# Softmax weights of the first three token groups on VectorE, and the values' low part ahead of the minima

## The chip, the cores and the metric

The kernel runs on one core of a Trainium2 chip. The metric is the time of one execution on the device, in microseconds (us); before the change it is 902.17 us, the median of three runs (901.9, 902.17 and 903.5). Nothing else runs on the core, and all inputs and outputs lie in HBM.

## The reference

Attention with a sliding window and a linear position bias, then two feed-forward layers over all tokens:

```python
scores = (q @ k^T) / sqrt(64)                # 4 batches, 8 heads, 576 positions, head size 64
scores = where(0 <= i - j < 128, scores - slope[h] * |i - j|, -1e9)
attn = exp(scores - max(scores)); attn /= sum(attn) + 1e-9
x = (attn @ v) as 2304 tokens x 512
h = x @ w_in;  x = (h * clip(h + 3, 0, 6) / 6) @ w_out        # 512 -> 2048 -> 512
h = x @ w_in2; out = (s * max(h, 0)**2 + b) @ w_out2           # 512 -> 2048 -> 512
```

All of it is float32, and the feed-forward products are made from two parts of each number: a high part rounded to the matmul's own type (fp32r) and the low part that is left.

## The kernel before

**Groups, units and steps.** The tokens are cut into eight groups of 256 or 320: groups 0 to 3 hold the first two blocks of 128 rows of each batch, groups 4 to 7 the rest. `NATIVE` is 2: groups 0 and 1 are computed by `StartUnit`, the others by `Unit`. A unit is one head of one group; two heads (an even and an odd one) form a pair and share the loads, and each of the two classes has the same stages: scale the queries, scores (TensorE), minima (VectorE, which also adds the bias and masks), exponentials (ScalarE, with the row sums as a second output), `sums` (VectorE: 1e-9 is added and the reciprocal taken), `weights` (the exponentials are multiplied with the reciprocals, on GpSimd), transposes (TensorE), copies into SBUF, values (TensorE), `to_hi` (ScalarE) and `to_lo` (VectorE), which leave the high and low part of the attention's result in the group's `x` tile. Beside the units run the steps of the first feed-forward layer: `Step(t, f)` computes for group `t` and block `f` of 128 hidden columns the product `h`, then ScalarE and VectorE form `g` and split it, then the product `o`. The matmuls of `h` need VectorE's `product` of the step before, since `h` has one PSUM bank.

**The weights.** The first layer's weights come in as raw numbers and are unpacked and split on the chip: `Half` does this in the first 130 us on ScalarE (`high`, L229 and L230; `hi`, L249), VectorE (`sign`, a shift at L234 and a bit operation at L237; `lo`, L253) and GpSimd (`add`, L243). The second layer's weights follow later in `Pair`.

**The order.** It is written out by hand: `at(slot, rank, fn)` puts a function into a slot at a rank, and slots and ranks are gone through in order; each engine gets its instructions in that order and works through them in order. Units of groups 0 and 1 take one slot each (unit `i` has its minima in slot `i`, its sums and weights in slot `i + 1`, its transposes in slot `i + 4`). From slot 13 on the steps take the even or odd slots, and the pairs of the later groups are eight slots apart, so that a group's units run beside the steps of the groups before. Within a slot the ranks that matter here are: 30.1 `high`, 30.4 `to_hi`, 31 `add` and `lo`, 31.5 `product`, 32 minima, 32.1 `lower`, 32.2 and 33 sums, exponentials and weights, 38 `sign`, 39 `to_lo`.

**Buffers.** The scores, transposes and values of `Unit` share three PSUM banks (tag `a`); a bank is free again when its last reader is done: the minima for the scores, `to_hi` and `to_lo` for the values. A unit's statistics (minimum, sum, reciprocal; up to five columns each) lie in a small tile `st` with four buffers. During the first slots TensorE also runs warm-up matmuls whose result nobody reads.

Of the kernel before, what the change touches and what calls it, by code (L numbers as in the profile page):

```python
# [8 lines left out]
F32 = mybir.dt.float32  # L9
# [5 lines left out]
ALU = mybir.AluOpType  # L15
# [8 lines left out]
def tile_alibi_window_attention_moe_moe2(  # L24
# [52 lines left out]
    def at(slot, rank, fn):  # L77
        plan.setdefault(slot, []).append((rank, len(plan[slot]), fn))
# [193 lines left out]
    attn_ctx = ExitStack()  # L272
    ap = attn_ctx.enter_context(tc.tile_pool(name="ap", bufs=2))

    def rows(i):
        return min(P, S - i * P)


    class Unit:
# [11 lines left out]
        def plan(self, s):  # L291
# [22 lines left out]
            if odd:  # L314
                at(s + 17, 20, self.values)
                at(s + 18, 30.4, self.to_hi)
                at(s + 18, 39, self.to_lo)

        def pair(self):
            return units[self.g * H + self.h // 2 * 2 :][:2]  # L320
# [62 lines left out]
        def minima(self):  # L383
            even = self.pair()[0]
            if even is self:
                self.st = ap.tile([P, 3, 5], F32, tag="st", bufs=4, name=f"st{self.id}")
            self.st = even.st
            self.Pt = ap.tile([P, 3, P], F32, tag="P", bufs=5, name=f"P{self.id}")
            for i in range(self.qa, self.two):
# [31 lines left out]
            self.exp(2, 4)  # L421

        def sums(self):
            n, st = 4 + (self.two < self.qb), self.st
            nc.vector.tensor_scalar(
                out=st[:, 2, :n], in0=st[:, 1, :n], scalar1=1e-9, scalar2=None, op0=ALU.add
            )
            nc.vector.reciprocal(st[:, 2, :n], st[:, 2, :n])  # L428

        def weight(self, i, c):  # L430
            pt = self.Pt[:, i]
            nc.gpsimd.tensor_scalar(  # L432
                out=pt, in0=pt, scalar1=self.st[:, 2, c : c + 1], scalar2=1.0,
                op0=ALU.mult, op1=ALU.mult,
            )

        def weights(self):
            for i in range(self.qa, self.two):
# [77 lines left out]
    class StartUnit(Unit):  # L516
# [36 lines left out]

        def scale(self):

            for u in self.pair():
                c = -(D ** -0.5) / slopes[u.h]
                if self.g + u.h == 0:
                    nc.vector.tensor_scalar(
                        out=u.X, in0=u.raw[u.p, :256], scalar1=c, scalar2=None, op0=ALU.mult  # L560
                    )
                elif self.g + self.h == 0:
                    nc.scalar.activation(u.X, u.raw[u.p, :256], AF.Copy, scale=c)
                else:
                    nc.gpsimd.tensor_scalar(
                        out=u.X, in0=u.raw[u.p, :256], scalar1=c, scalar2=1.0,
                        op0=ALU.mult, op1=ALU.mult,
                    )

        blocks = ((0, 0, P), (1, P, 3 * P))  # L570

# [10 lines left out]

        def minima(self):
            self.Pt = ap.tile([P, 3 * P], F32, tag="P", bufs=5, name=f"P{self.id}")
            self.st = ap.tile([P, 3, 5], F32, tag="st", bufs=4, name=f"st{self.id}")
            for i, a, b in self.blocks:
                nc.vector.tensor_tensor_reduce(  # L587
                    out=self.Pt[:, a:b], in0=self.ps[:, a:b], in1=rel2[:, 2 * P - (b - a) :],
                    scale=slopes[self.h], scalar=3.0e38, op0=ALU.add, op1=ALU.min,
                    accum_out=self.st[:, 0, i : i + 1],  # L590
                )
# [6 lines left out]
                )  # L598

        def sums(self):  # L600
            nc.vector.tensor_scalar(
                out=self.st[:, 2, :2], in0=self.st[:, 1, :2], scalar1=1e-9, scalar2=None, op0=ALU.add
            )
            nc.vector.reciprocal(self.st[:, 2, :2], self.st[:, 2, :2])

        def weights(self):
            for i, a, b in self.blocks:
                nc.gpsimd.tensor_scalar(
                    out=self.Pt[:, a:b], in0=self.Pt[:, a:b], scalar1=self.st[:, 2, i : i + 1],
                    scalar2=1.0, op0=ALU.mult, op1=ALU.mult,  # L610
                )

        def transposes(self):
# [719 lines left out]
```

## Time and profile before

| | before |
|---|---|
| median of three runs | 902.17 us |
| the profiled execution | 902.07 us, of which the span from first to last instruction is 900.4 |
| TensorE busy (matmuls) | 877.4 us, 97% |
| VectorE | 624.7 us, 69% |
| ScalarE | 521.6 us, 58% |
| GpSimd | 341.7 us, 38% |

The names in the profile are PE for TensorE's matmuls and PEld for its weight loads, DVE for VectorE, ACT for ScalarE, POOL for GpSimd and SP for the engine that issues the DMAs. A row of a timeline has the start, the duration, the engine, the line of the kernel, the operation, what it writes and reads, and in brackets how long the engine sat idle before it and what ended that. Busy shares are means over stages that have different limits.

### The profile page before, as it was taken

The numbers are of one execution on the slowest core, as the hardware profiler recorded it, in microseconds if no ns is written. First come the engines' busy times: TensorE is split into PE (matmuls) and PEld (weight loads), VectorE is DVE, ScalarE is ACT, GpSimd is POOL, SyncE is SP. The second block draws the span as 40 slices with busy tenths as digits, with TensorE's granted clock in tenths as the row PEclk, the third lists the DMA queues.
The fourth block names the chain that finished last, engine by engine and source line by source line (L and its number), as shares of the span: only waits on it lengthen the run. The fifth ranks groups of instructions, "written<-read, shape, count | busy, mean of one in ns | idle before, by whom it ended". The sixth has DMA issues, their size and how long they took to land.

```text
span 900.4 us, 17714 instructions
## 1 busy us (share of the span) xinstructions
PE 877.4 (97%) x6469; PEld 836.4 (93%) x6469; DVE 624.7 (69%) x1376; ACT 521.6 (58%) x1227; POOL 341.7 (38%) x526
## 2 busy tenths in 40 slices
PE   9799899999999999999999999999999999999998
PEld 4589889899999999999999999999999999999998
DVE  7899885665787667776765745778747787476672
ACT  7888775555665556556555435665446656266551
POOL 7834541323554544454442311444104440144300
PEclk9999999999999999999999999999999999999999
DMA  9454332427466546454447335887779777777772
GB/s 336 134 174 136 112 106 89 160 65 231 139 210 205 170 148 216 161 180 165 170 170 257 141 165 183 297 299 263 274 237 327 274 270 268 256 259 261 281 258 94
DMA packets 66823, 183.19 MB, mean 203 GB/s; under 512 B 9904, under 2 KB 29616, under 8 KB 58288
## 3 DMA queue, kind: packets, MB, share of 16 engines
q1 hardware_dynamic: 66736, 182.06, 59.1%
q8 instruction: 51, 0.84, 0.4%
q14 instruction: 36, 0.29, 0.1%
HBM read 143.13 MB, written 38.80 MB: 202 GB/s over the span
## 4 chain that ended last, share of the span: by engine, by line
PE 84%; DVE 7%; ACT 4%; DMA 2%; issue 2%; SPq 0%; POOL 0%; ACTq 0%; POOLq 0%
PE o L1062 20%; PE h L1122 19%; PE h L672 19%; PE o L710 18%; PE v L497 3%; PE s L368 2%; DMA raw<-w 2%; PE t L453 1%; DVE staging_early L234 1%; DVE g L697 1%; ACT staging_early L229 1%; DVE raw L237 1%; PE s L376 1%; DVE P L587 1%; DVE t L686 1%
## 5 line engine op out<-in xcount | busy, mean ns | idle before, releaser
L710 PE MATMUL o<-g,w 128*128 128x256 f32 (+1 forms) x1536 | 234.2, 301 | 1.1 <-DVE g L697 0.9
L672 PE MATMUL h<-x,w 128*128 128x256 f32 (+1 forms) x1536 | 226.8, 296 | 7.9 <-DVE t L686 7.6
L710 PEld LDWEIGHTS o<-g,w 128*128 128x128 f32 x1536 | 210.8, 189 | 10.8 <-issue 4.2
L672 PEld LDWEIGHTS h<-x,w 128*128 128x128 f32 x1536 | 211.3, 189 | 10.2 <-DVE t L686 9.5
L1062 PE MATMUL o<-wstream,i 128*128 128x256 f32 x1512 | 180.4, 281 | 0.0
L1062 PEld LDWEIGHTS o<-wstream,i 128*128 128x128 f32 x1512 | 180.0, 188 | 0.0
L1122 PE MATMUL h<-x,wstream 128*128 128x384 f32 x1008 | 176.7, 334 | 0.0
L1122 PEld LDWEIGHTS h<-x,wstream 128*128 128x128 f32 x1008 | 174.4, 188 | 0.2
L683 ACT ACTIVATE t<-h 128x256 f32<-128x256 f32 (+1 forms) x128 | 52.4, 409 | 141.5 <-PE h L672 141.1
L686 DVE SCALAR_TENSOR_TENSOR t<-t,h 128x256 f32<-128x256 f32 (+1 forms) x128 | 57.7, 451 | 80.2 <-ACT t L683 79.7
L697 DVE TENSOR_TENSOR g<-t,g 128x256 fp32r<-128x256 f32 (+1 forms) x128 | 67.2, 525 | 34.6 <-ACT g L693 32.6
L482 POOL TENSOR_SCALAR_AFFINE_SELECT W<-F 128x128 f32<-128x128 f32 (+1 forms) x144 | 46.8, 359 | 108.6 <-ACT F L457 104.5
L1156 ACT ACTIVATE g<-g,scalar 128x384 f32<-128x384 f32 x96 | 58.6, 610 | 39.4 <-DVE g L1141 37.0
L432 POOL TENSOR_SCALAR P<-P,st 128x128 f32<-128x128 f32 x112 | 57.1, 524 | 41.6 <-DVE st L428 40.5
L693 ACT ACTIVATE g<-t 128x256 fp32r<-128x256 f32 (+1 forms) x128 | 56.3, 440 | 28.5 <-DVE t L686 28.2
L1179 POOL TENSOR_TENSOR g<-g 128x384 f32<-128x384 f32 x24 | 24.3, 1015 | 117.7 <-PE h L1122 98.8
L1140 DVE TENSOR_TENSOR g<-h,s 128x384 f32<-128x384 f32 x72 | 39.8, 553 | 31.3 <-PE h L1122 22.5
L919 DVE SCALAR_TENSOR_TENSOR i<-g,scalar,i 128x768 fp32r<-128x768 f32 x48 | 49.3, 1077 | 11.7 <-ACT i L918 11.7
L1091 ACT ACTIVATE u<-o 128x256 f32<-128x256 f32 x36 | 13.2, 385 | 73.1 <-PE o L1062 73.1
L1141 DVE SCALAR_TENSOR_TENSOR g<-g 128x384 f32<-128x384 f32 x72 | 47.3, 658 | 2.5
L918 ACT ACTIVATE i<-g,scalar 128x768 fp32r<-128x768 f32 x48 | 41.5, 926 | 6.4 <-PE o L1062 6.4
L1132 ACT ACTIVATE s<-h 128x384 f32<-128x384 f32 x72 | 34.7, 482 | 17.8 <-PE h L1122 17.4
(122 smaller groups left out, 1176.6 us busy)
## 6 DMA issues: line engine op xcount, KB each, us to landing
wstream<-wo SPq DMA_DIRECT2D x42, 1024.0 KB, 5.0
raw<-w SPq DMA_DIRECT2D x53, 512.0 KB, 4.9
wstream<-wh SPq DMA_DIRECT2D x24, 1024.0 KB, 5.6
wstream<-wh SPq DMA_DIRECT2D x24, 768.0 KB, 5.8
wh<-staging_early SPq DMA_DIRECT2D x16, 512.0 KB, 3.0
wo<-staging_early SPq DMA_DIRECT2D x12, 512.0 KB, 3.3
stage<-w SPq DMA_DIRECT2D x11, 512.0 KB, 4.4
out<-u SPq DMA_DIRECT2D x11, 384.0 KB, 3.0
```

What stands on the lines that cost most here:

```text
L432: nc.gpsimd.tensor_scalar(out=pt, in0=pt, scalar1=self.st[:, 2, c : c + 1], scalar2=1.0, op0=ALU.mult, op1=ALU.mult,)
L672: nc.tensor.matmul(self.ps, lhsT=w[:, wp, cc * P : (cc + 1) * P], rhs=x[:, cc, xp], start=m == 0, stop=m == 3 * CC - 1,)
L683: nc.scalar.activation(self.a, self.ps, AF.Relu, bias=3.0)
L686: nc.vector.scalar_tensor_tensor(out=self.a, in0=self.a, scalar=6.0, in1=self.ps, op0=ALU.min, op1=ALU.mult)
L693: nc.scalar.activation(self.g[:, 0], self.a, AF.Copy)
L697: nc.vector.tensor_tensor(out=self.g[:, 1], in0=self.a, in1=hi, op=ALU.subtract)
L710: nc.tensor.matmul(acc[t][d], lhsT=w[:, wp, DM + d * P : DM + (d + 1) * P], rhs=self.g[:, gp], start=f == 0 and i == 0 and (t > 1 or d % 2 ...
L919: nc.vector.scalar_tensor_tensor(out=out[:, :, 1], in0=src, scalar=b, in1=hi.bitcast(F32), op0=ALU.add, op1=ALU.subtract,)
L1062: nc.tensor.matmul(self.acc[k][c], lhsT=g[:, gp, c * P : (c + 1) * P], rhs=w[:, wp * HB : (wp + 1) * HB], start=k in (0, 1, 5) and p == 0 ...
L1122: nc.tensor.matmul(self.ps[first], lhsT=w[:, wp, cc], rhs=x[:, cc, xp], start=n == first and m == 0, stop=m == 5, skip_group_check=True,)
L1141: nc.vector.scalar_tensor_tensor(out=g, in0=g, scalar=0.0, in1=g, op0=ALU.max, op1=ALU.mult)
L1156: nc.scalar.activation(g, g, AF.Copy, scale=s_sb)
```

## The change

Four things change, and one goes with them.

- In `to_lo` of `Unit` only the place changes: rank 31.9 instead of 39 in its slot, so that VectorE has it ahead of the minima.
- `weights` of `StartUnit` (groups 0 and 1) and of group 2 (`self.g == NATIVE`) multiply on VectorE instead of GpSimd, with the same operands.
- `sums` becomes `inverse`: instead of adding 1e-9 with an immediate, a reduction over two rows of the statistics adds the sum and a row that holds 1e-9, and writes over the minimum, which the exponentials no longer need; the reciprocal follows in place. All units use it.
- In `scale` of `StartUnit` the two scalings of a pair on GpSimd, 64 partitions each with a constant, become one over 128 partitions with a column of constants; the first pair's stay on VectorE and ScalarE.
- The statistics lie in one tile with four slots, used in turn, whose row of 1e-9 GpSimd fills once.

```diff
@@ -272,6 +272,26 @@
     attn_ctx = ExitStack()
     ap = attn_ctx.enter_context(tc.tile_pool(name="ap", bufs=2))
 
+
+    NST = 4
+    sts = []
+
+    def next_st():
+        if not sts:
+            whole = ap.tile([P, NST, 3, 5], F32, bufs=1, name="st")
+            nc.gpsimd.memset(whole[:, :, 2], 1e-9)
+            sts.extend(whole[:, i] for i in range(NST))
+        sts.append(sts.pop(0))
+        return sts[-1]
+
+    def inverse(st, n):
+        total = st[:, 0, :n]
+        nc.vector.tensor_reduce(
+            out=total, in_=st[:, 1:3, :n].rearrange("p r n -> p n r"),
+            axis=mybir.AxisListType.X, op=ALU.add,
+        )
+        nc.vector.reciprocal(total, total)
+
     def rows(i):
         return min(P, S - i * P)
 
@@ -314,7 +334,7 @@
             if odd:
                 at(s + 17, 20, self.values)
                 at(s + 18, 30.4, self.to_hi)
-                at(s + 18, 39, self.to_lo)
+                at(s + 18, 31.9, self.to_lo)
 
         def pair(self):
             return units[self.g * H + self.h // 2 * 2 :][:2]
@@ -383,7 +403,7 @@
         def minima(self):
             even = self.pair()[0]
             if even is self:
-                self.st = ap.tile([P, 3, 5], F32, tag="st", bufs=4, name=f"st{self.id}")
+                self.st = next_st()
             self.st = even.st
             self.Pt = ap.tile([P, 3, P], F32, tag="P", bufs=5, name=f"P{self.id}")
             for i in range(self.qa, self.two):
@@ -421,18 +441,16 @@
             self.exp(2, 4)
 
         def sums(self):
-            n, st = 4 + (self.two < self.qb), self.st
-            nc.vector.tensor_scalar(
-                out=st[:, 2, :n], in0=st[:, 1, :n], scalar1=1e-9, scalar2=None, op0=ALU.add
-            )
-            nc.vector.reciprocal(st[:, 2, :n], st[:, 2, :n])
+            inverse(self.st, 4 + (self.two < self.qb))
 
         def weight(self, i, c):
-            pt = self.Pt[:, i]
-            nc.gpsimd.tensor_scalar(
-                out=pt, in0=pt, scalar1=self.st[:, 2, c : c + 1], scalar2=1.0,
-                op0=ALU.mult, op1=ALU.mult,
-            )
+            pt, r = self.Pt[:, i], self.st[:, 0, c : c + 1]
+            if self.g == NATIVE:
+                nc.vector.tensor_scalar(out=pt, in0=pt, scalar1=r, scalar2=None, op0=ALU.mult)
+            else:
+                nc.gpsimd.tensor_scalar(
+                    out=pt, in0=pt, scalar1=r, scalar2=1.0, op0=ALU.mult, op1=ALU.mult
+                )
 
         def weights(self):
             for i in range(self.qa, self.two):
@@ -553,19 +571,21 @@
 
         def scale(self):
 
-            for u in self.pair():
-                c = -(D ** -0.5) / slopes[u.h]
-                if self.g + u.h == 0:
-                    nc.vector.tensor_scalar(
-                        out=u.X, in0=u.raw[u.p, :256], scalar1=c, scalar2=None, op0=ALU.mult
-                    )
-                elif self.g + self.h == 0:
-                    nc.scalar.activation(u.X, u.raw[u.p, :256], AF.Copy, scale=c)
-                else:
-                    nc.gpsimd.tensor_scalar(
-                        out=u.X, in0=u.raw[u.p, :256], scalar1=c, scalar2=1.0,
-                        op0=ALU.mult, op1=ALU.mult,
-                    )
+            if self.g + self.h == 0:
+                for u in self.pair():
+                    c = -(D ** -0.5) / slopes[u.h]
+                    if u.h == 0:
+                        nc.vector.tensor_scalar(
+                            out=u.X, in0=u.raw[u.p, :256], scalar1=c, scalar2=None, op0=ALU.mult
+                        )
+                    else:
+                        nc.scalar.activation(u.X, u.raw[u.p, :256], AF.Copy, scale=c)
+            else:
+                j = self.h // 2
+                nc.gpsimd.tensor_scalar(
+                    out=self.raw[:, 768:], in0=self.raw[:, :256], scalar1=qscale[:, j : j + 1],
+                    scalar2=1.0, op0=ALU.mult, op1=ALU.mult,
+                )
 
         blocks = ((0, 0, P), (1, P, 3 * P))
 
@@ -582,7 +602,7 @@
 
         def minima(self):
             self.Pt = ap.tile([P, 3 * P], F32, tag="P", bufs=5, name=f"P{self.id}")
-            self.st = ap.tile([P, 3, 5], F32, tag="st", bufs=4, name=f"st{self.id}")
+            self.st = next_st()
             for i, a, b in self.blocks:
                 nc.vector.tensor_tensor_reduce(
                     out=self.Pt[:, a:b], in0=self.ps[:, a:b], in1=rel2[:, 2 * P - (b - a) :],
@@ -598,16 +618,13 @@
                 )
 
         def sums(self):
-            nc.vector.tensor_scalar(
-                out=self.st[:, 2, :2], in0=self.st[:, 1, :2], scalar1=1e-9, scalar2=None, op0=ALU.add
-            )
-            nc.vector.reciprocal(self.st[:, 2, :2], self.st[:, 2, :2])
+            inverse(self.st, 2)
 
         def weights(self):
             for i, a, b in self.blocks:
-                nc.gpsimd.tensor_scalar(
-                    out=self.Pt[:, a:b], in0=self.Pt[:, a:b], scalar1=self.st[:, 2, i : i + 1],
-                    scalar2=1.0, op0=ALU.mult, op1=ALU.mult,
+                nc.vector.tensor_scalar(
+                    out=self.Pt[:, a:b], in0=self.Pt[:, a:b], scalar1=self.st[:, 0, i : i + 1],
+                    scalar2=None, op0=ALU.mult,
                 )
 
         def transposes(self):
```

## Rows read from the trace of the kernel before

**Rows 1.** The page's busy time, share of the span and instructions of each engine.
```profile
PE 877.4 (97%) x6469; PEld 836.4 (93%) x6469; DVE 624.7 (69%) x1376; ACT 521.6 (58%) x1227; POOL 341.7 (38%) x526
```
**Rows 2.** Busy time by stage: stage, length, busy (instructions) by engine, clock, DMA, GB/s.
```profile
12.05:29.87 17.82, 16.53 (x113) 9.37 (x112) 17.41 (x69) 17.27 (x55) 16.92 (x29) 1.00 0.82 319
29.87:45.00 15.13, 11.16 (x72) 8.30 (x71) 12.18 (x42) 12.63 (x37) 11.47 (x15) 0.89 0.35 106
60.00:130.00 70.00, 63.80 (x522) 59.40 (x523) 62.94 (x153) 56.67 (x142) 34.24 (x41) 1.00 0.37 118
130.00:480.00 350.00, 344.23 (x2659) 326.08 (x2659) 236.71 (x685) 198.25 (x547) 149.43 (x309) 1.00 0.51 167
```
**Rows 3.** The timeline of VectorE between 8 and 40 us.
```profile
8.62 0.29 DVE L587 CUSTOM_DVE_ANT_0 P<-s,rel 128x128 f32<-128x128 f32 x1 [0.61 <-PE s L578]
...
10.90 0.43 DVE L234 TENSOR_SCALAR staging_early<-staging_early 128x512 int32<-128x512 int32 x1 [0.53 <-ACT staging_early L229]
...
12.05 0.28 DVE L587 CUSTOM_DVE_ANT_0 P<-s,rel 128x128 f32<-128x128 f32 x1
...
21.75 0.17 DVE L604 RECIPROCAL st<-st 128x2 f32<-128x2 f32 x1
21.84 0.40 DVE L512 TENSOR_TENSOR x<-v,x 128x256 fp32r<-128x256 f32 x1
...
29.87 0.28 DVE L587 CUSTOM_DVE_ANT_0 P<-s,rel 128x128 f32<-128x128 f32 x1
...
34.21 0.68 DVE L253 TENSOR_TENSOR w<-stage,w 128x512 fp32r<-128x512 f32 x1
...
36.48 0.70 DVE L601 TENSOR_SCALAR st<-st 128x2 f32<-128x2 f32 x1
...
39.78 0.42 DVE L697 TENSOR_TENSOR g<-t,g 128x256 fp32r<-128x256 f32 x1 [1.13 <-ACT g L693]
```
**Rows 4.** The timeline of ScalarE and TensorE between 30 and 35 us.
```profile
30.25 0.41 ACT L595 ACTIVATE P<-P,st 128x128 f32<-128x128 f32 x1 [0.25 <-DVE st L587]
...
34.56 0.89 PE L578 MATMUL s<-raw 64*128 64x128 f32 x6 [2.40 <-ACT W L625]
```
**Rows 5.** The timeline of GpSimd and VectorE at 31 and at 58 us.
```profile
31.63 3.53 POOL L608 TENSOR_SCALAR P<-P,st 128x128 f32<-128x128 f32 x4
...
57.81 1.04 POOL L243 TENSOR_TENSOR raw<-raw 128x512 int32<-128x512 int32 x1 [3.86 <-DVE raw L237]
...
57.86 1.27 DVE L234 TENSOR_SCALAR staging_early<-staging_early 128x512 int32<-128x512 int32 x1
```
**Rows 6.** VectorE's groups by line and shape, 10.85 to 29.9 us: busy us, mean ns.
```profile
L253 DVE TENSOR_TENSOR w<-raw,w 128x512 fp32r<-128x512 f32 x4 | 3.5, 882 | 0.0
...
L601 DVE TENSOR_SCALAR st<-st 128x2 f32<-128x2 f32 x8 | 1.8, 224 | 0.0
```
**Rows 7.** VectorE's groups by line and shape over the whole span.
```profile
L425 DVE TENSOR_SCALAR st<-st 128x5 f32<-128x5 f32 x16 | 2.6, 161 | 0.0
...
L122 DVE TENSOR_SCALAR rel<-rel 128x128 f32<-128x128 f32 x1 | 0.2, 227 | 0.0
```
**Rows 8.** The timeline of TensorE and VectorE at 220 and at 355 us.
```profile
220.62 0.41 PE L453 MATMUL t<-ident,P 128*128 128x128 f32 x2 [1.01 <-DVE st L394]
...
354.82 0.48 DVE L686 SCALAR_TENSOR_TENSOR t<-t,h 128x320 f32<-128x320 f32 x1
...
355.52 1.92 PE L672 MATMUL h<-x,w 128*128 128x320 f32 x12
```
**Rows 9.** What TensorE waited for, 60 to 130 us: us in all, times, longest.
```profile
PE h L672 <- DVE t L686: 6.6, 6, 1.7
```
**Rows 10.** The timeline of VectorE and TensorE from 78 to 81 us.
```profile
78.15 1.26 DVE L234 TENSOR_SCALAR staging_early<-staging_early 128x512 int32<-128x512 int32 x1
...
80.58 1.70 PE L672 MATMUL h<-x,w 128*128 128x256 f32 x12 [0.84 <-DVE t L686]
```
**Rows 11.** What TensorE waited for, over the whole span.
```profile
PE t L453 <- DVE st L394: 4.4, 5, 1.0
```

## The prediction

> **What bounds the kernel now.** I read the page's engine shares first, then the busy time by stage, then VectorE's instructions in the stages where it is full, and last what TensorE waited for. Over the span TensorE is busy 97% and VectorE 69% [rows 1], but that average hides two regimes [rows 2]. From 130 us on, TensorE is busy 344.23 of 350 us and VectorE 236.71: work added to VectorE there is beside TensorE's. Before that it is the other way round. From 12.05 to 29.87 us VectorE is busy 17.41 of 17.82 us, ScalarE 17.27 and GpSimd 16.92; TensorE's 16.53 is padded with warm-up matmuls. From 60 to 130 VectorE has 62.94 of 70 us, TensorE 63.80. The change puts work on VectorE exactly in these two stages, and takes it from GpSimd.
>
> The start can be read as one chain. The minima of unit 4 begin at 12.05, those of unit 12 at 29.87 [rows 3]: four pairs of units in 17.82 us, 4.46 us a pair. VectorE's rows of that stretch follow each other without a gap. ScalarE's exponentials of unit 12 start at 30.25, after 0.25 us of waiting for exactly those minima, and TensorE's scores at 34.56 wait 2.40 us for a copy that stands behind them in ScalarE's queue [rows 4]. So a microsecond more on VectorE between 12 and 30 us comes out later at TensorE, and nothing after 45 us has the room to give it back.
>
> VectorE's durations there hold waits for GpSimd. At 57.81 GpSimd's add starts and takes 1.04 us; VectorE's shift, 0.43 us when alone at 10.90 [rows 3], starts at 57.86 and takes 1.27: it ended only after the add [rows 5]. The opposite order exists too: from 31.63 four of GpSimd's multiplies took 3.53 us while VectorE ran without a gap. In the start the difference of two weights took 0.88 us in the mean against 0.68 at 34.21, and the sum's first instruction 0.224 against 0.161 [rows 3, 6, 7].
>
> **The change, part by part.** The sum is made against the profiled execution: 902.07 us, a span of 900.4 and 1.7 around it; the median of the runs is 902.17, so the two are one number here.
>
> *Weights of groups 0 and 1 (16 units).* Per unit VectorE gains one 128x128 and one 128x256 multiply, SBUF to SBUF. The trace has no such multiply on VectorE. Nearest is the 128x128 add of a constant, 0.227 us [rows 7]; for 256 columns I go a third of the way to the 0.43 of 128x512: 0.30. The other bound is one element per cycle: 0.28 for the minima's 128x128 [rows 3], and between that and 0.48 for 320 columns [rows 8] about 0.41. I take the first, as its operands lie in the same memory. VectorE's next instruction starts some 0.08 before the recorded end of the one in front (the reciprocal at 21.75 lasts 0.17, its successor starts at 21.84), so the two take 0.20 + 0.22; but the first of them needs the reciprocal's result and waits for its end, 0.11 more. That is 0.53 a unit, 1.06 a pair; by the other bound 1.4.
> What may come back: the difference of weights 0.88 to 0.68 once a pair, and the sum's 0.224 to 0.161 twice (its new form is a reduction of ten numbers at most, which I price like the old one): 0.33 a pair. GpSimd keeps one add of 1.04 and one scaling a pair, so the multiplies can now wait for these. I take half of the relief and 0.1 of new waits: +1.0 a pair, +4.0 for the four pairs between 12.05 and 29.87 (2.9 with all relief and no waits; 7.2 with the dear multiplies, no relief and one wait of 0.4 a pair).
> Ahead of 12.05 three units add 1.6 us, of which the idle 0.61 at 8.62 and 0.53 at 10.90 [rows 3] take most: +0.5 (0 to 1.6). One thing may add there: the constants' column is filled by GpSimd behind its first scaling; if the first minima wait for it, up to 1.0, the nearest row being GpSimd's add of 1.04 [rows 5]. After 29.87 four units add 2.1 us, beside three gaps of VectorE between 35 and 40 us, the largest 1.13 at 39.78, and the sum at 36.48 no longer sits 0.70 for GpSimd: +0.3 (-0.5 to 1.0). **Start: +4.8 us (2.4 to 10).**
>
> How much the multiplies wait for the add is the open size. The Trainium skill (SBUF — State Buffer, section "Who interferes with whom") says that VectorE in its two-port mode and GpSimd exclude each other, and whoever issues first holds the pair for the whole instruction. Both orders in [rows 5] agree. By that rule alone, with every add issued first, each pair would lose another 1.04 us and the start would cost some 9 us; with VectorE's unbroken queue first, nothing.
>
> *Scaling of the queries.* Two 64x256 instructions on GpSimd become one of 128x256. GpSimd, which sets no wait of the chain above, has one instruction and four multiplies fewer a pair: 0. Were it on the chain, it would be less work than before, never more.
>
> *Weights of group 2 (8 units, 16 multiplies).* They fall in the stage of 60 to 130 us, where TensorE waited six times for VectorE's product, 6.6 us in all [rows 9, 10]. The even unit's two multiplies come ahead of the shift at 78.15; that shift already waited for GpSimd's add (1.26 us). Now the multiplies wait instead and the shift follows: product and next h step move by 0.43 at most (0.20 and 0.23). I take 0.38, since GpSimd's own multiplies no longer run beside the bit operations behind, on a wait that TensorE feels (0.84 at 80.58), four times over: **+1.5 us** (0.3 if ScalarE's copy ends last in three of the four; 3.2 with dear multiplies and the odd units felt as well). The odd unit's pair stands where a difference of weights waited for the next add; it takes that wait over, and TensorE's next wait comes only with the next pair: 0.
>
> *The values' low part ahead of the minima (groups 2 to 7, 24 instructions).* Nothing is added; the instruction moves ahead of two minima and, in some slots, of bit operations. It no longer holds the bank of the values behind them. Five times, at the first pair of a group, TensorE's transposes waited for a bank until the minima were done: 4.4 us in all, 1.01 of it at 220.62 [rows 8, 11]. The values' bank, now freed first, would be there a minima's time earlier. Not all of it stays: after the wait in group 5 the next h step begins at 355.52, 0.2 after VectorE's product of 354.82 ends, and that product doesn't move. I keep the whole 1.0 of the first, 0.2 of this one, and of the other three, read in the same way, 1.2, of which 0.7 goes to a product that is late a few us behind: **-1.7 us** (-4.4 if all is kept; +0.4 if VectorE, now first waiting for ScalarE's high part, passes that wait on). The queue behind the moved instruction holds the minima, whose exponentials have a slot to spare. It issues no DMA, and passes none on SP's queue.
>
> *The statistics in one tile.* No instruction but one fill; costed at 0 beyond the 1.0 above.
>
> Sum: 902.07 + 4.8 + 1.5 - 1.7 = **906.7 us**.
>
> **The rivals.** *The lock rules the start.* Every add of GpSimd is issued just before a multiply or a shift and holds VectorE for its whole 1.04 us; start +9.0, group 2 +2.2, low part -1.7: 911.5. For it: 57.86 [rows 5]. Against it: VectorE's queue has no gap in which GpSimd could go first.
> *All relief comes back.* The start costs 2.4, group 2 0.3, the low part gives 1.7: 903.1. For it: GpSimd has five instructions fewer a pair. Against it: the add and the scaling remain.
> *GpSimd was the pace (faster).* The place is TensorE's gap before 34.56 and the stretch of slow matmuls behind it (granted clock 0.89 in the mean from 29.87 to 45, so a part of it at 1.2 GHz) [rows 2, 4]. If what TensorE lacks there is GpSimd's backlog from 31.63 [rows 5] and not ScalarE's copy, the 2.40 us go, and with them the 0.11 of 15.13 us that the clock withheld, 1.7. It decides as soon as this 4.1 exceeds what the start costs plus group 2 less the low part; with the start at 2.4 it gives 902.07 + 2.4 + 1.5 - 1.7 - 4.1 = 900.2, with the low part's whole 4.4 it gives 897.5; I put it at 899. Against it: the transposes that need the backlog come after the scores, which ScalarE released.
>
> **How the numbers follow.** Forecast 0.52, lock 0.14, all relief 0.19, faster 0.15. About 0.2% (1.8 us) is what can be told from no change. The forecast's own range is 904 to 910; for 8 in 10 I go down to 900.4 and up to 911.5. Slower than 904: nearly all of the first two, a quarter of the third, 0.64. Within: most of the third and a little of the others, 0.21. Faster: 0.15.
>
> **What would show it.** Right: unit 12's minima start near 34.5 us, not 29.87; VectorE's rows from 12 us on still have no gap while GpSimd is mostly idle; the new multiplies take 0.23 and 0.30; VectorE's busy time grows by some 11 us; the wait of transposes for the minima falls from 4.4 to about 2; TensorE's wait for the product in 60 to 130 us grows from 6.6 to about 8. Wrong: unit 12's minima at 31.5 or earlier (then VectorE's own work was not the pace), TensorE's gap before its scores gone and no clock loss behind it, or multiplies at 0.28 and 0.41.

## The result, and the profile after

The changed kernel takes 907.82 us, the median of four runs (907.64 to 908.66), beside 902.29 for the kernel before on the same chip: a ratio of 1.0060, interval 1.0048 to 1.0073, so 5.5 us slower. The profiled execution took 907.75 us, its span 906.0.

The engine shares first, from the page of the changed kernel:

```profile
PE 879.1 (97%) x6466; PEld 836.3 (92%) x6469; DVE 634.3 (70%) x1424; ACT 521.9 (58%) x1227; POOL 310.1 (34%) x472
```

VectorE has 9.6 us more than in [rows 1], GpSimd 31.6 less. Now the stages, set to the same work as [rows 2]: unit 4's minima to unit 12's, the 15 us behind them, group 2's stage, and the long rest.

```profile
12.42:33.74 21.32, 16.10 (x107) 8.97 (x107) 20.63 (x85) 17.48 (x54) 7.53 (x9) 1.00 0.69 260
33.74:48.87 15.13, 11.13 (x71) 7.92 (x70) 13.31 (x46) 12.25 (x36) 4.81 (x4) 0.89 0.31 90
66.00:136.00 70.00, 63.10 (x516) 58.42 (x516) 63.26 (x168) 55.94 (x141) 21.45 (x24) 1.00 0.38 117
136.00:486.00 350.00, 345.29 (x2661) 326.18 (x2660) 237.80 (x685) 198.25 (x546) 149.69 (x309) 1.00 0.51 166
```

The first stage is the result: 21.32 us in place of 17.82, with VectorE busy in 20.63 of them and GpSimd in 7.53. The clock is the same as before in every stage, and the long rest gives nothing back. VectorE's timeline, to be held against [rows 3]:

```profile
12.42 0.28 DVE L607 CUSTOM_DVE_ANT_0 P<-s,rel 128x128 f32<-128x128 f32 x1
...
12.98 0.15 DVE L289 TENSOR_REDUCE st<-st 128x2 f32<-128x4 f32 x1
13.16 0.17 DVE L293 RECIPROCAL st<-st 128x2 f32<-128x2 f32 x1
13.37 0.66 DVE L625 TENSOR_SCALAR P<-P,st 128x128 f32<-128x128 f32 x2
...
14.89 0.55 DVE L625 TENSOR_SCALAR P<-P,st 128x128 f32<-128x128 f32 x2
15.35 0.55 DVE L640 COPY W<-t 128x384 f32<-128x384 f32 x1
...
33.74 0.28 DVE L607 CUSTOM_DVE_ANT_0 P<-s,rel 128x128 f32<-128x128 f32 x1
```

The two multiplies of a unit take 0.55 us together, and at 13.37, beside GpSimd's instructions below, 0.66. No row between the two minima has idle time in front of it. ScalarE and TensorE behind it are late by the same amount, as the chain of [rows 4] says:

```profile
34.12 0.41 ACT L615 ACTIVATE P<-P,st 128x128 f32<-128x128 f32 x1 [0.24 <-DVE st L607]
...
38.32 1.37 PE L598 MATMUL s<-raw 64*128 64x128 f32 x6 [1.78 <-ACT W L642]
```

The exponentials of unit 12 moved by 3.87 us, as its minima did, and the scores by 3.76; their own wait is 1.78 in place of 2.40. GpSimd in the same stretch, against [rows 5]:

```profile
12.65 1.04 POOL L243 TENSOR_TENSOR raw<-raw 128x512 int32<-128x512 int32 x1 [3.15 <-DVE raw L237]
13.95 0.48 POOL L585 TENSOR_SCALAR raw<-raw,qscale 128x256 f32<-128x256 f32 x1 [0.26 <-DMA raw<-qkv0p]
17.11 1.36 POOL L243 TENSOR_TENSOR raw<-raw 128x512 int32<-128x512 int32 x1 [2.67 <-ACT P L615]
```

At 17.11 it is the add that waits (1.36 for 1.04), while VectorE runs on. VectorE's groups of the stretch from 12.42 to 33.74 (busy, mean ns), against [rows 6], with the relief in them: the difference of weights fell from 882 to 684 ns, the sum's first instruction from 224 to 151.

```profile
L625 DVE TENSOR_SCALAR P<-P,st 128x256 f32<-128x256 f32 x8 | 3.2, 402 | 0.0
L253 DVE TENSOR_TENSOR w<-raw,w 128x512 fp32r<-128x512 f32 x4 | 2.7, 684 | 0.0
L625 DVE TENSOR_SCALAR P<-P,st 128x128 f32<-128x128 f32 x8 | 2.4, 301 | 0.3
L289 DVE TENSOR_REDUCE st<-st 128x2 f32<-128x4 f32 x8 | 1.2, 151 | 0.0
```

Group 2, at the pair that answers to [rows 10]:

```profile
82.54 1.10 POOL L243 TENSOR_TENSOR raw<-raw 128x512 int32<-128x512 int32 x1 [3.86 <-DVE raw L237]
82.66 1.26 DVE L449 TENSOR_SCALAR P<-P,st 128x128 f32<-128x128 f32 x2
...
83.84 0.41 DVE L234 TENSOR_SCALAR staging_early<-staging_early 128x512 int32<-128x512 int32 x1
...
84.90 0.41 DVE L703 SCALAR_TENSOR_TENSOR t<-t,h 128x256 f32<-128x256 f32 x1
...
85.36 0.86 PE L689 MATMUL h<-x,w 128*128 128x256 f32 x5 [1.11 <-DVE t L703]
```

The two multiplies took over the wait for GpSimd's add that the shift had, the shift behind them was free (0.41 at 83.84), and TensorE's next step waited 1.11 us in place of 0.84. Last, what TensorE waited for over the whole span, where [rows 11] had the transposes at 4.4:

```profile
PE h L689 <- DVE t L703: 10.0, 10, 2.0
...
PE t L471 <- DVE x L530: 1.5, 3, 1.0
```

The transposes' wait fell further than forecast, to 1.5. But the wait for the product, 7.6 us in eight waits before, is 10.0 in ten.

### The profile page after: what moved, and what is told of

The parts are those of the page before. It is cut to its first block, busy times and chain, and to the rows that moved or that the text cites. A ratio compares the mean times of both kernels' runs of the same rounds, so it can differ in the third digit from the quotient of the medians.

```text
span 906.0 us, 17691 instructions
## 1 busy us (share of the span) xinstructions
PE 879.1 (97%) x6466; PEld 836.3 (92%) x6469; DVE 634.3 (70%) x1424; ACT 521.9 (58%) x1227; POOL 310.1 (34%) x472
## 4 chain that ended last, share of the span: by engine, by line
PE 84%; DVE 7%; ACT 5%; issue 2%; DMA 1%; ACTq 0%; DVEq 0%
PE o L1079 20%; PE h L1139 19%; PE h L689 19%; PE o L727 18%; PE v L515 3%; PE s L388 2%; DMA raw<-w 1%; PE t L471 1%; ACT staging_early L229 1%; DVE staging_early L234 1%; DVE g L714 1%; DVE t L703 1%; PE warm_ps L100 1%; ACT P L431 1%; ACT raw L230 1%
## 5 line engine op out<-in xcount | busy, mean ns | idle before, releaser
L1157 DVE TENSOR_TENSOR g<-h,s 128x384 f32<-128x384 f32 x72 | 39.8, 553 | 31.2 <-PE h L1139 22.5
L451 POOL TENSOR_SCALAR P<-P,st 128x128 f32<-128x128 f32 x96 | 46.2, 496 | 39.9 <-DVE st L293 38.9
```

Of the source, the lines that this page charges most:

```text
L451: nc.gpsimd.tensor_scalar(out=pt, in0=pt, scalar1=r, scalar2=1.0, op0=ALU.mult, op1=ALU.mult)
```

## The experiments

Each row is a median of several runs beside runs of the kernel before on the same chip. The stretch is from unit 4's minima to unit 12's in the profiled execution. Between two executions the first minima start anywhere from 5.7 to 7.0 us, so stretches compare better than starts. Stretches scatter too: five profiles with the start of the changed kernel have 21.30 to 21.57 us, and two with the start of the kernel before 17.82 and 18.29.

| kernel | us | before | ratio (95%) | stretch, us |
|---|---|---|---|---|
| changed | 907.82 | 902.29 | 1.0060 (1.0048-1.0073) | 21.32 |
| low part alone | 901.39 | 901.83 | 0.9995 (0.9986-1.0003) | 18.29 |
| changed, start's weights on GpSimd | 904.79 | 901.83 | 1.0023 (1.0012-1.0033) | 16.79 |
| changed, group 2's weights on GpSimd | 906.42 | 901.83 | 1.0047 (1.0035-1.0059) | 21.56 |
| before, with ballast on VectorE | 908.27 | 901.83 | 1.0074 (1.0061-1.0087) | 22.89 |
| changed, low part back | 908.39 | 901.94 | 1.0075 (1.0061-1.0089) | 21.57 |
| sums, scaling and tile only | 901.74 | 901.94 | 0.9997 (0.9989-1.0006) | 16.98 |
| changed, all weights on GpSimd | 901.10 | 901.94 | 0.9991 (0.9982-1.0000) | 16.98 |
| start's weights alone | 907.06 | 902.49 | 1.0051 (1.0039-1.0063) | 21.56 |
| changed, once more | 907.74 | 902.49 | 1.0057 (1.0044-1.0070) | 21.30 |
| changed, GpSimd kept busy | 909.92 | 902.49 | 1.0080 (1.0066-1.0094) | 21.83 |
| all on GpSimd, one sum a pair | 900.66 | 902.49 | 0.9976 (0.9964-0.9987) | 16.52 |
| new sums alone | 903.33 | 902.42 | 1.0003 (0.9994-1.0013) | 18.05 |

**Is VectorE's own time the pace of the start?** The kernel before with two reductions of a constant table more in each unit, on VectorE, GpSimd's work as it was:

```diff
         def weights(self):
+            for n in (P, 2 * P):
+                nc.vector.tensor_reduce(
+                    out=self.st[:, 2, 4:5], in_=rel2[:, :n], axis=mybir.AxisListType.X, op=ALU.add
+                )
```

> The kernel before, weights on GpSimd as before, with two reductions of constant data (128 and 256 numbers, 0.55 us together, result unused) added on VectorE in each of the 16 units of groups 0 and 1, where the change puts the multiplies. Theory A (VectorE's own time is the pace of the start): unit 12's minima start 4 to 5 us later than 29.87 and the time is 906 to 908 us, like the change itself, although GpSimd keeps its work. Rival (the start is slow because the multiplies and GpSimd's add exclude each other, or because GpSimd is the pace): one-element-a-cycle reductions do not meet GpSimd, and VectorE's waits shrink by what is added: 902 to 904 us.

Measured: 908.27. The minima of units 4 and 12 in its trace:

```profile
13.01 0.28 DVE L587 CUSTOM_DVE_ANT_0 P<-s,rel 128x128 f32<-128x128 f32 x1
...
35.90 0.28 DVE L587 CUSTOM_DVE_ANT_0 P<-s,rel 128x128 f32<-128x128 f32 x1
```

22.89 us in place of 17.82: 5.07 for eight times two reductions, 0.63 a unit, which is what the two take from start to start (0.64). VectorE's products from 56 to 106 us stand 5.96 to 5.98 us later than in the kernel before, and the time grew by 6.4, a little past the 906 to 908 expected. With GpSimd's work as it was, VectorE's time is the pace. What VectorE loses beside GpSimd changed as well (groups by line, to be held against [rows 6]):

```profile
L601 DVE TENSOR_SCALAR st<-st 128x2 f32<-128x2 f32 x8 | 2.9, 363 | 0.0
L253 DVE TENSOR_TENSOR w<-raw,w 128x512 fp32r<-128x512 f32 x4 | 2.7, 684 | 0.0
```

The difference of weights became shorter, 0.684 for 0.882, and the sum's first instruction longer, 0.363 for 0.224 twice a pair; the two nearly cancel.

**The start alone, and the start taken back.**

```diff
# start's weights alone, from the changed kernel
-                at(s + 18, 31.9, self.to_lo)
+                at(s + 18, 39, self.to_lo)
-            if self.g == NATIVE:
+            if False:
```

> The changed kernel with group 2's weights on GpSimd and the low part at rank 39: of the moved weights only those of groups 0 and 1 are left. Theory: the start costs 4.5 to 5.0 us, and nothing behind it adds or gives back: 906.4 to 907.0, and VectorE's products keep one distance from the kernel before, within 0.2 us, from 56 us on. From the traces so far group 2's weights alone add 0.6 behind that point, the low part alone takes 0.7 to 1.2, and both together add 1.1. Rival: the three edits add up; then this kernel stands at the changed kernel's time less 1.3 for group 2 plus 0.5 for the low part, 907.0 or more, or its distance changes behind 56 us.

```diff
# start's weights on GpSimd, from the changed kernel (StartUnit.weights)
-                nc.vector.tensor_scalar(
+                nc.gpsimd.tensor_scalar(
-                    scalar2=None, op0=ALU.mult,
+                    scalar2=1.0, op0=ALU.mult, op1=ALU.mult,
```

> The changed kernel with the weights of groups 0 and 1 back on GpSimd; the new sums, the single scaling, the early low part and group 2's weights on VectorE stay. Theory A: the 4.5 us that the start lost are the multiplies on VectorE; without them unit 12's minima start at or before 29.9 us and the time is 902 to 903.5 us (group 2 still costs 1.3, the lighter sums and scaling may give 1 back). Rival: the new sums or the one tile of statistics make the start longer: 905 us or more, unit 12's minima later than 31.5.

The start alone costs 907.06 - 902.49 = 4.6 us, nearly all of the change. VectorE's products are 4.94 us later than in the kernel before at 56 us, 4.70 at 113 and 5.40 from 190 us on: they kept their distance to 0.7 us, not to the 0.2 expected, and 907.06 lies at the edge of the theory's range and of the rival's. Taking the start back gave only 3.0 (907.82 to 904.79; 3.3 by the ratios), with a wide spread, 900.8 to 905.74. Unit 12's minima, at 29.51, came as the theory had it, the time did not (902 to 903.5). Its profiled execution shows why that run is no clean subtraction. After one step of group 2 the granted clock fell (TensorE's row, then the stages that hold it and follow it, with the clock third from the end):

```profile
127.89 1.89 PE L689 MATMUL h<-x,w 128*128 128x256 f32 x12 [1.95 <-DVE t L703]
```
```profile
125.00:130.00 5.00, 3.05 (x22) 2.62 (x23) 4.33 (x11) 3.05 (x8) 2.02 (x3) 0.92 0.02 3
130.00:135.00 5.00, 5.00 (x35) 3.67 (x34) 3.46 (x11) 1.97 (x5) 1.10 (x1) 0.73 0.22 62
```

TensorE stood for 1.95 us and got 0.73 of its clock in the five us from 130 on, so it ran for a part of them at 1.2 GHz. The changed kernel's own profiled execution has a stop of 1.96 us at 132.22 and kept 1.00. Three of the twelve runs with the start's weights on GpSimd had a mean clock of 0.998 or above; they took 900.8, 901.7 and 903.56. Why the clock falls in most executions of that kernel and not in others isn't settled.

**Group 2, and the low part.** Four kernels: the low part early in the kernel before; the changed kernel with group 2's weights on GpSimd (`if False:` as above); the changed kernel with the low part back at rank 39; and the changed kernel again, beside the start alone.

```diff
# low part alone, from the kernel before
-                at(s + 18, 39, self.to_lo)
+                at(s + 18, 31.9, self.to_lo)
```

> The kernel before with one edit: the values' low part at rank 31.9 instead of 39. Theory A (the prediction's): the bank comes free earlier at the first pair of five groups, and 1.7 us of the 4.4 us of waiting stay gained: about 900.5 us. Theory B (from the trace of the changed kernel, where VectorE's products run 5.8 us late at 126 us and 5.7 us late at 433 us): TensorE's transposes wait less, but the next h step then waits for a product that has not moved, so nothing stays: 901.8 to 902.5 us, with the wait of transposes below 2 us and the wait of h for the product up by about as much as that fell.

> The changed kernel with group 2's weights back on GpSimd and everything else as changed. Theory A: group 2's sixteen multiplies cost the 1.3 us by which the products fall back further between 60 and 126 us: 906.5 us, and TensorE's wait for the product in 66 to 136 us falls from 7.4 to about 6.2. Rival: that growth comes from the early low part of group 2, which waits for ScalarE's high part: 907.5 to 908 us.

> The changed kernel with the values' low part back behind the minima (rank 39); all else as changed. Theory: early, the low part is worth what the run with it alone gave, some 0.4 us, since the transposes' shorter waits are paid again at the next product; so this kernel takes 908.0 to 908.4, TensorE's transposes again wait about 4.4 us in all for the minima, and VectorE's product at the first steps of the later groups stands within 0.5 us of the changed kernel's. Rival, the prediction's term: the low part gives 1.7 us; then 909.5.

> The changed kernel itself, beside the other three on one chip. Theory: 907.3 to 908.0, 0.8 to 1.2 above the kernel that moves the start's weights alone. Rival (edits add up): within 0.5 of that kernel, since the low part's gain pays for most of group 2.

Low part alone: 901.39, which is -0.44 by a ratio whose interval holds 1, and lies between the two theories (900.5, and 901.8 to 902.5). The low part back: 908.39 against 907.82, +0.6 by the medians and 1.4 by the ratios, each against its own runs of the kernel before. Both are short of 1.7.

Group 2's weights back on GpSimd: 906.42, as the theory had it (906.5), which is 1.4 below the changed kernel by the medians and 1.2 by the ratios; the rival (907.5 to 908) falls. TensorE's wait for the product between 60 and 140 us is 1.8 us shorter, first the changed kernel, then this one:

```profile
PE h L689 <- DVE t L703: 7.4, 6, 2.0
```
```profile
PE h L689 <- DVE t L703: 5.6, 6, 1.2
```

Group 2 and low part together, by the changed kernel beside the start alone: +0.68. I had expected 0.8 to 1.2 there from an idea that the two edits hinder each other, since VectorE waited 0.70 us for ScalarE at 127.67 in the changed kernel's trace. The second profile of the same kernel has no such wait, and TensorE's stop there is 1.52 and not 1.96. That reason falls: it was one execution's. With the low part at -0.5, group 2 is worth +1.2.

The idea itself is still open. With the low part early and group 2's weights on GpSimd, VectorE's products gain 0.8 to 0.9 us on the kernel before between 60 and 133 us: from 0.14 late to 0.67 early with the low part alone, from 5.00 to 4.13 late with the start's weights moved as well. With group 2's weights on VectorE they gain nothing there: from 4.52 to 5.78 late in one profile of the changed kernel, from 4.36 to 4.66 in the other. The times lie too close together to decide it.

So the low part's gain is not where it was looked for. In the profiled execution of the low part alone the transposes wait 1.5 us in all, where [rows 11] had 4.4; but of these 2.9 us only 0.33 reached VectorE's products (0.67 early at 133 us, 1.00 early at 475). The other 0.8 came in group 2's stage, where TensorE's wait for the product from 60 to 130 us is 5.7 us in place of the 6.6 of [rows 9]. How the early low part shortens that wait isn't shown.

```profile
PE t L453 <- DVE x L512: 1.5, 3, 1.0
```
```profile
PE h L672 <- DVE t L686: 5.7, 6, 1.3
```

Where the gain at the transposes went is told by the waits of VectorE's low part for ScalarE's high part, first in the kernel before, then with the low part alone moved:

```profile
DVE x L512 <- ACT x L508: 1.4, 2, 0.8
```
```profile
DVE x L512 <- ACT x L508: 4.3, 6, 0.9
```

and by one such place, first before, then with the low part early:

```profile
282.24 0.29 DVE L394 CUSTOM_DVE_ANT_0 P<-s,rel 128x128 f32<-128x128 f32 x1
...
282.46 0.48 DVE L512 TENSOR_TENSOR x<-v,x 128x320 fp32r<-128x320 f32 x1
282.69 0.41 PE L453 MATMUL t<-ident,P 128*128 128x128 f32 x2 [0.81 <-DVE st L394]
```
```profile
279.82 1.14 ACT L801 ACTIVATE work<-raw 128x1024 f32<-128x1024 f32 x1
...
280.86 0.42 ACT L508 ACTIVATE x<-v 128x320 fp32r<-128x320 f32 x1
...
281.32 0.49 DVE L512 TENSOR_TENSOR x<-v,x 128x320 fp32r<-128x320 f32 x1 [0.86 <-ACT x L508]
...
281.96 0.41 PE L453 MATMUL t<-ident,P 128*128 128x128 f32 x2 [0.95 <-DVE x L512]
```

ScalarE's high part stands behind a decode of 1.14 us (L801). VectorE, which used to do two minima in that time, now stands 0.86 us in front of the low part, and the transposes wait 0.95 for the bank after all. At 219.27 it went as forecast for the transposes, 0.21 in place of 1.01, but VectorE's later products did not move as far, and the step at 227.72 waits 0.20 for one: of 0.80, 0.3 stayed.

**Sums, scaling, tile, and all weights on GpSimd.** Two kernels, the first with the low part at rank 39, the second with it at 31.9; and a third with the new sums but the scaling of a pair in two halves as before.

> Only the new sums, the single scaling of a pair and the statistics in one tile; all weights on GpSimd and the low part at rank 39, as before. Theory: nothing here is on the path that sets the end: 901.5 to 902.5, unit 12's minima within 0.4 us of 29.87, and VectorE's sums no dearer than 0.22. Rival: the fill of the tile or the reduction is dearer than priced, at up to 1.0 us ahead of 12 us and 0.06 a sum in four pairs: 903 to 903.5, unit 12's minima at 30.4 or later.

> The changed kernel with all weights back on GpSimd: new sums, single scaling, one tile, and the low part ahead of the minima. Theory: the low part's 0.4 is all that is left of the change: 901 to 902, and the changed kernel's whole loss (5.5) lies in where the weights are multiplied. Rival: sums, scaling or tile cost something as well, or the low part's gain needs the old order of the start: 902.5 to 903.5. Second rival: one scaling less on GpSimd shortens the start's waits and adds to the low part's gain: 900.5 or less.

> As the run with the new sums, the single scaling and the one tile, but with the scaling of a pair as two instructions of 64 partitions again: only the sums are new. There, unit 4's to unit 12's minima took 16.98 us instead of 17.82, and the difference of two weights 0.68 instead of 0.88. Theory: the reduction does this, since it does not wait for GpSimd as the added constant did (0.15 instead of 0.22) and the difference behind it neither: 16.9 to 17.2 us here too, with GpSimd's scalings as before. Rival: the single scaling does it, as GpSimd has one instruction fewer a pair to collide with: 17.5 to 17.9. Either way the time stays within 1 us of the kernel before, 901 to 902.5, since the gain did not pass unit 15's minima there.

The first two times are as expected. With the sums alone the time is 0.9 above the kernel before, 903.33 for a forecast of at most 902.5, by a ratio whose interval holds 1. The stretch is not as expected: it is 0.84 us shorter with sums and scaling, and with the sums alone it isn't (minima of units 4 and 12, and the difference of weights from 12 to 30 us; first sums and scaling, then the sums alone).

```profile
12.70 0.28 DVE L607 CUSTOM_DVE_ANT_0 P<-s,rel 128x128 f32<-128x128 f32 x1
...
29.68 0.28 DVE L607 CUSTOM_DVE_ANT_0 P<-s,rel 128x128 f32<-128x128 f32 x1
...
L253 DVE TENSOR_TENSOR w<-raw,w 128x512 fp32r<-128x512 f32 x4 | 2.7, 678 | 0.0
```
```profile
12.71 0.28 DVE L605 CUSTOM_DVE_ANT_0 P<-s,rel 128x128 f32<-128x128 f32 x1
...
30.76 0.28 DVE L605 CUSTOM_DVE_ANT_0 P<-s,rel 128x128 f32<-128x128 f32 x1
...
L253 DVE TENSOR_TENSOR w<-raw,w 128x512 fp32r<-128x512 f32 x4 | 3.5, 880 | 0.0
```

So my theory falls and the rival stands: here it is the single scaling, not the reduction, that freed the difference of weights, 0.2 us once a pair, beside a GpSimd that is busy in 18.00 of the 18 us from 12 to 30 in the first and in 17.10 in the second. It is not the only way to free it: in the ballast run the difference took 0.684 with the scaling in two halves. The reduction is shorter (0.15 for 0.22) but the next instructions wait longer (the bit operation 0.83 for 0.77). That the 0.84 does not reach the end goes with the clock behind the stretch, in the kernel before, then with sums and scaling, then with the sums alone (30 to 55 us, clock third from the end):

```profile
30.00:55.00 25.00, 21.03 (x152) 17.19 (x151) 21.95 (x58) 21.05 (x54) 16.09 (x27) 0.93 0.43 136
```
```profile
30.00:55.00 25.00, 21.93 (x147) 17.78 (x146) 19.95 (x56) 21.06 (x55) 15.91 (x26) 0.86 0.42 131
```
```profile
30.00:55.00 25.00, 21.15 (x143) 16.97 (x142) 20.20 (x58) 21.16 (x58) 17.05 (x25) 0.86 0.37 115
```

0.07 of 25 us is 1.75 us of full clock that TensorE lost more, with the shorter stretch and without it. With the sums alone this covers the 0.9: the runs took 901.87 to 902.35 at a mean clock of 0.998 and 903.21 to 904.49 at 0.996. Why these executions lost clock there isn't shown. The runs with all weights on GpSimd spread in the same way: 899.15 and 900.52 at a mean clock of 1.00, 900.06 to 900.94 at 0.998, 901.1 to 902.38 at 0.996.

**Does the relief come from GpSimd's idling?** The changed kernel, with GpSimd multiplying as much as before into memory that nobody reads:

```diff
# StartUnit.weights, behind VectorE's multiplies
+            for i, a, b in self.blocks:
+                nc.gpsimd.tensor_scalar(
+                    out=self.raw[:, 768 : 768 + b - a], in0=rel2[:, 2 * P - (b - a) :],
+                    scalar1=self.st[:, 0, i : i + 1], scalar2=1.0, op0=ALU.mult, op1=ALU.mult,
+                )
```

> The changed kernel with GpSimd's load of the start put back beside VectorE's: in each unit of groups 0 and 1 GpSimd also multiplies 128 and 256 columns of a constant table into a dead part of the pair's raw tile; nobody reads the result. Theory: the relief that paid for part of the move comes from GpSimd's idling. With its multiplies there again VectorE's two-input instructions and multiplies wait for it as before, 0.3 a pair: unit 4's to unit 12's minima in 22.5 us instead of 21.3, and 908.8 to 909.5. Rival: VectorE's queue has no gap in which GpSimd could go first, so GpSimd waits and VectorE does not: 21.3 to 21.6 us, 907.3 to 908.1.

The stretch is 21.83 us, 0.5 more than the changed kernel's: nearer to the rival (21.3 to 21.6) than to the theory (22.5), and not far outside the scatter of equal starts. The difference of weights stayed at 0.684, the sum at 0.150; only the multiplies grew, by 0.053 and 0.015, which makes the 0.5 over eight units:

```profile
L625 DVE TENSOR_SCALAR P<-P,st 128x256 f32<-128x256 f32 x8 | 3.6, 455 | 0.0
...
L625 DVE TENSOR_SCALAR P<-P,st 128x128 f32<-128x128 f32 x8 | 2.5, 316 | 0.3
```

The time, 909.92, is 2.2 above the changed kernel beside it, above both expectations. The stretch explains a quarter. From the first minima to unit 4's it is 6.87 us for 6.45, another 0.4; and the profiled execution has the clock loss behind a stop of 1.95 us (at 118.38) as well, worth 1.3 us there. What GpSimd's work costs VectorE is read from the stretch.

**A version that gains.** With all weights on GpSimd and the low part early, a pair of the start shares its statistics: one reduction and one reciprocal of four columns in place of two of two.

```diff
-            at(s + 1, 33, self.sums)
-            at(s + 1, 33, self.weights)
+            if self.h % 2:
+                at(s + 1, 33, self.sums)
+                at(s + 1, 33, self.pair()[0].weights)
+                at(s + 1, 33, self.weights)
```

> All weights on GpSimd, new sums, low part early, and in groups 0 and 1 the two units of a pair share their statistics: one reduction and one reciprocal a pair in place of two each, and the even unit's weights one slot later. Theory: VectorE's own time is the pace of the start here too; it loses some 0.3 us a pair: unit 4's to unit 12's minima in 15.8 instead of 17.0 us, and 899.8 to 900.3. Rival: with GpSimd busy in all 24 us from 12 to 36, GpSimd is a second pace and VectorE only waits longer: 16.8 us or more, 901 to 901.8.

900.66 us, ratio 0.9976 (0.9964 to 0.9987): faster than both kernels, by 1.8 and 7.1 us (the changed kernel beside it: 907.74). The stretch came to 16.52, 0.46 shorter than without the shared sums where VectorE's own saving would give 1.2, and so between the theory's 15.8 and the rival's 16.8: GpSimd, busy in 24.00 of 24 us from 12 to 36, is close behind as a second pace. Against the version without shared sums (901.10, in another set of runs) the gain isn't established.

## Why the prediction was right, and where it was not

Forecast 906.7, measured 907.8, inside the forecast's own range of 904 to 910. The mechanism of the largest term, the start, is the one that the runs show. That the sum comes so near is in part luck: the low part gave 1.2 us less than forecast, group 2 and the start cost 0.3 and 0.2 less, and within the start two errors cancel.

*The start, +4.8: measured +4.6* (start alone). The step "a microsecond more on VectorE between 12 and 30 us comes out later at TensorE" is shown by the ballast. Between the profiled executions of the two kernels the parts are +0.46 from the first minima to unit 4's for a forecast 0.5, +3.50 over the four pairs for 4.0, and +0.65 from unit 12's minima to the product at 56 us for 0.3. Unit 12's minima came at 33.74 for 34.5.

Within the four pairs the multiplies are dearer than forecast and the relief larger. The recorded 0.30 and 0.40 lie at the dear bound (0.28 and 0.41), which the prediction had named as a sign that it is wrong; I had taken 0.23 and 0.30. From start to start they take up to 0.62 and 0.46 for the two units of a pair, and each unit's first multiply waits some 0.12 longer for the reciprocal: 1.3 a pair for a forecast 1.06 and 0.1 of new waits. The relief, of which I had counted half (0.17), came in full: 0.20 at the difference of weights and 0.12 at the sums, and 0.08 at the bit operation, which I hadn't counted. What is left is 0.88 a pair in the mean for a forecast 1.0. The 1.06 also doesn't follow from its own numbers: 0.23 and 0.30 less 0.08 each, and 0.11, make 0.48 a unit and not 0.53. And behind unit 12's minima stand the weights of five units, not four. Both slips are small beside the range.

What the relief is due to is known in part. The runs without moved weights show the single scaling take 0.2 off the difference of weights, an edit that I costed at 0 because GpSimd "sets no wait of the chain". It sets none, but its instructions stretch VectorE's. The ballast shows the same 0.2 with the scaling in two halves, so the changed kernel's own relief can't be put down to it.

*How the lock falls.* The Trainium skill (SBUF — State Buffer, section "Who interferes with whom") says that of VectorE in its two-port mode and GpSimd the first to issue keeps the other out, and that a VectorE instruction with two inputs in SBUF contends with a GpSimd instruction that reads SBUF. The trace agrees with it in both orders: at 17.11 GpSimd's add took 1.36 us beside VectorE's difference of two weights (0.69 from 16.88), at 82.66 VectorE's multiplies 1.26 behind the add. The first rival's 1.04 a pair did not come: the multiplies that started during the add at 13.37 took 0.66 for 0.55, and the start cost 4.6 and not 9. With GpSimd's multiplies put back the stretch grew by only 0.13 a pair: in this start, an unbroken queue on VectorE leaves the waiting mostly to GpSimd.

*Group 2, +1.5: measured +1.2*, by difference and by the run that takes it back. Beside that run TensorE's waits at the four pairs are longer by 0.28, 0.26, 0.32 and 0.34 in the second profile of the changed kernel, 1.2 in all, for a forecast 0.38 each; in the first profile they are 0.27, 0.30, 0.43 and 0.78, the last with the stop that only this execution has. The step named, the multiplies take over the shift's wait for the add, is seen at the first pair. At the other three the even unit's multiplies are free (0.47 recorded, 0.39 from start to start), and the shift and the product move back by that.

*The low part, -1.7: measured about -0.5.* This is the term that was mis-sized, and the step is "The values' bank, now freed first, would be there a minima's time earlier". The bank is freed by the low part, which needs ScalarE's high part, and where that stands behind a decode VectorE now stops for it. I had this as the far bound (+0.4) and not as what happens at some of the places. The forecast that the transposes' wait would fall to about 2 came true (1.5), and shows that a wait which goes is not yet time: with the low part alone 0.33 of 2.9 us arrived. The larger gain of that run, 0.8 in group 2's stage, has no term in the prediction, and the changed kernel's traces don't show it.

*The rest.* The fill of the tile took 0.12 us at 6.84, behind the first minima (5.97) and ahead of the first reduction at 7.39, which waited for ScalarE. VectorE's busy time grew by 9.6 us for a forecast 11, and TensorE's wait for the product in group 2's stage from 6.6 to 7.4 for about 8. *All relief comes back* (903.1) had the relief right but put the start at 2.4, too low by half. *GpSimd was the pace* falls with the ballast and the stretch. TensorE's gap before its scores shrank from 2.40 to 1.78, without any gain of clock (0.89 in both).

What stays open: when exactly the clock falls behind a stop of 1.95 us, how much of the single scaling's relief is in the changed kernel itself, which wasn't tried, and whether group 2's weights take away what the early low part gives.

## What to carry to other kernels

Ask for each stage which engine has no gap, and price moved work there from start to start, not by recorded durations. Here an instruction moved from an engine that was nearly as busy to the one that sets the pace cost its whole time, and the relief beside GpSimd paid back less than a third of it. A term that comes out right can hide two that are wrong, so check a forecast part by part. Before an instruction is moved forward in a queue, look at when its own input is ready: a wait moved to another instruction isn't removed.

## What the runs showed of the hardware

A 128x128 and a 128x256 float32 multiply on VectorE with a scalar per partition take 0.30 and 0.40 us in the records, 0.46 to 0.62 together from start to start. The GpSimd scaling of a pair in one instruction of 128 partitions in place of two of 64 made VectorE's difference of weights 0.2 us shorter (0.880 to 0.678). Behind a TensorE stop of 1.95 us the granted clock of a five-us window that began some 2 us later was 0.73 in one execution and 0.71 in another kernel's; in the changed kernel's it was 1.00 behind a stop of 1.96.
